# One ring of six PSUM banks, and a DFT-47 on 64x64 tiles with constants per frequency slot

## The chip, the cores and the metric

The kernel runs on one core of a Trainium2 chip. What counts is the device time of one execution in microseconds (us), the median of several runs.

The core's engines work side by side, each through its own queue in order, and wait for one another by semaphores. TensorE (PE in the rows; PEld is its weight load) multiplies; VectorE (DVE), ScalarE (ACT) and GpSimd (POOL) do the elementwise work; SyncE (SP) issues most transfers, and POOL issues some. A transfer or an instruction that waits holds up all that stands behind it in the same queue.

## What is computed

The input x is 8 x 3008 x 256. Along the sequence of 3008 it goes through a real FFT, a complex 256x256 product with bias and a soft threshold, and the inverse FFT. What comes out goes through a feed-forward layer whose gate is h cos(h):

```python
X = np.fft.rfft(x, axis=1)
Yr = Xr @ w_r - Xi @ w_i + b_r
Yi = Xr @ w_i + Xi @ w_r + b_i
Yr = np.sign(Yr) * np.maximum(np.abs(Yr) - lam, 0.0)
Yi = np.sign(Yi) * np.maximum(np.abs(Yi) - lam, 0.0)
y = np.fft.irfft(Yr + 1j * Yi, n=3008, axis=1)
h = y @ w_in            # 256 -> 2048
g = h * np.cos(h)
out = g @ w_out         # 2048 -> 256
```

## The kernel before

**The transform.** Since 3008 = 64 * 47, the FFT is a DFT-64 and then a DFT-47, with indices permuted on the host so that no twiddle factors stand between them. For each batch b there are three stages. `stage_a(b)` loads x in six chunks (tile `xt`), folds mirrored halves on POOL into sums (`xe`) and differences (back into `xt`), and makes the DFT-64 in three bursts of matmuls into `pa`, two chunks to a burst. ACT copies `pa` out to `ao`, and the result goes to DRAM (`scr1`). `stage_b(b)` works on four quarters q of eight frequency slots each:

- `load(q)` brings the tile `at` back from `scr1`.
- `forward(q)` makes the DFT-47: 16 matmuls of K = 24 by M = 32, 512 columns wide, into four banks `pb`. Each of the four h (cosine or sine part of real or imaginary part) has one block of 24 rows, and one and the same 24x32 constant serves all slots. DVE transposes the four banks back over `at`, and the tile goes through DRAM (`scrF`) to the tile `z`, which brings channels onto the partitions.
- `combine(q)` has POOL add and subtract the four parts of `z` to make real and imaginary spectrum (`x`, L519), patch slot 0 when q is 0 (L524 to L527), and multiply by signs (L532). ACT casts each to float32r (`Xh`, L513), DVE or POOL takes the rest (`Xl`), and the sum of both parts, for a three-product complex multiplication, gets the same treatment.
- `wmix(q)` is that complex product: 36 matmuls into six banks `pw` one after another, with bias and threshold on ACT and DVE; its `fold` brings the result through `tr` and DRAM (`scrT`) to the tile `y`.
- `inverse(q)`, for b > 0 through `spread(q)`, makes the inverse DFT-47 into four banks `pi`, copied by ACT to `bo` and stored to `scr2`.

`stage_c(b, t)` loads one of six column tiles back (`bt`), makes the inverse DFT-64 into `pc` and splits the result in two float32r parts, `xTh` and `xTl`.

**The feed-forward layer.** `moe_step(b, t, f)` runs for 8 batches, 6 column tiles and 16 blocks f of 128 hidden channels, 768 steps in all. One step has six matmuls into `ph`; then ACT and DVE in turn make h cos(h) (L812, L813, L815, L816: `u`), ACT casts (L817: `gh`), and DVE or, for two f of four, POOL takes the rest (`gl`, helpers `rest` L286 and `rest_pool` L283). `second` is the product with w_out: six matmuls into `po`, four of `gh` and two of `gl`; it is written three steps behind (`SKEW = 3`, four buffers of `gh` and `gl`).

**Order.** The Fourier stages of batch b+1 (and `stage_a` of b+2) are generators; each `moe_step` of batch b pulls from them twice, as many yields as a budget allows (`A_COST`, `B_COST`, `C_COST`, from `PAIR`, `QUAD`, `READ`). `weave` puts `stage_a` between the yields of `stage_b`, one yield to every `A_EVERY`; `GAP` sets the distance of the last `stage_c`. A scheduler then sets the order on each engine.

**Banks.** Two of the eight PSUM banks hold `po`. Tag "h" has two banks for `ph`, tag "f" four for all Fourier products (`BANKS`, L41):

```python
ph = ps.tile([128, 512], F32, tag="h", name="ph", bufs=BANKS["h"])
```

A matmul that starts a tile waits until the readers of the tile that had the bank before are through. So a step's `ph` waits for the last reader, L816, of the `ph` two steps back. `burst` makes the first of a group of matmuls wait for all four banks at once, so that the rest runs without waits.

**Staging buffers.** `stage_out` gives one of three buffers (tag "ao") to `ao`, `bo` and `ob`; `tr` has a buffer of its own. `z`, `at` and `y` have one buffer each.

Of the kernel before, what the change touches and what calls it, by code (L numbers as in the profile page):

```python
# [38 lines left out]
GAP = 7  # L39
A_EVERY = 5  # L40
BANKS = dict(f=4, h=2)  # L41
PAIR, QUAD, READ = 1.15, 1.25, 0.3
# [30 lines left out]
def _constants():  # L73
# [66 lines left out]
    cs = np.zeros((4, 32, 32))  # L140
    rows = np.arange(24).reshape(2, 6, 2).transpose(1, 0, 2).reshape(-1)
    cs[:2, :24, :24] = C[rows, :24]
    cs[2:, :24, :24] = S[rows, :24]
    cs = cs.reshape(128, 32)
    c_sig = np.concatenate([np.ones((48, 32)), sig.T]).astype(np.float32)
    c_ff = np.concatenate([f1, ei, fa, cs], 1).astype(np.float32)
# [4 lines left out]
    return [np.ascontiguousarray(a) for a in (c_sig, c_f3, c_ff, c_if, c_iw, c_sgn)]  # L151
# [3 lines left out]
def tile_body(ctx: ExitStack, tc, x, w_r, w_i, b_r, b_i, w_in, w_out,  # L155
              c_sig, c_f3, c_ff, c_if, c_iw, c_sgn, out):
# [10 lines left out]
    ff = cp.tile([128, 352], F32, name="ff")  # L167
# [68 lines left out]
    def split_f64(hi, lo, raw):  # L236
# [53 lines left out]
    banks = []  # L290

    def fps(name):
        if "pro" in pool:
            if not banks:
                banks.extend("fhf")
            tag = banks.pop(0)
            return ps.tile([128, 512], F32, tag=tag, name=name, bufs=BANKS[tag])
# [6 lines left out]
    def drained(p, ins):  # L304

        for q, readers in (side if "pro" in pool else ring)[-8:]:
            if q is p:
                readers.append(ins.ins)
# [16 lines left out]
    def burst(m, calls, loads=()):  # L325
# [5 lines left out]
        kept, n = (side, 2) if "pro" in pool else (ring, BANKS["f"])  # L331
# [70 lines left out]
    def stage_a(b):  # L402
# [20 lines left out]
        for c0 in range(0, 6, at_once):  # L423
# [10 lines left out]
            for c in cs:  # L434
# [9 lines left out]
                del ld[c], ev[c]  # L444
                load(c + 2)
            yield PAIR * at_once


    def stage_b(b):
# [17 lines left out]

        def load(q):
            if b and q < 4:
                at[q] = wk.tile([128, 2048], F32, tag="at", name="at", bufs=1), []  # L470
                for h in range(4):
                    ins = nc.sync.dma_start(at[q][0][32 * h:32 * h + 24].rearrange("j (s d) -> j s d", s=8),
                                            scr1[b][h // 2, :, 8 * q:8 * q + 8, h % 2])
                    at[q][1].append(ins)
                    if b == 1 and q == 0:
                        behind(ins, mark["pc"], "first tile")
# [486 lines left out]
```

## Time and profile before

| | us |
|---|---|
| median of 3 runs | 2814.15 (2811.34 to 2817.79) |
| the profiled execution, its own time | 2816.3 |
| its span, first to last instruction | 2814.5 |
| PE busy in the span | 2657.7 (94%) |
| DVE busy | 1901.3 (68%) |
| ACT busy | 1668.3 (59%) |
| POOL busy | 1204.0 (43%) |

The mean granted TensorE clock of the execution is 0.976 of full speed. Up to about 120 us the Fourier stages of batch 0 run alone; from then to about 2480 us feed-forward steps and Fourier stages run side by side; the rest is the feed-forward layer of the last batch. Each of the seven batches 1 to 7 has four `pb` bursts, four `pi` bursts and 24 `pw` products; there are 21 `pa` bursts. A busy span in a row is what the record says of one instruction; matmuls overlap, so what one costs PE is read from the start of one to the start of the next.

### The profile page before, as it was taken

What the parts mean: (1) busy time and instruction counts of PE and PEld (TensorE: products, weight loads), DVE (VectorE), ACT (ScalarE), POOL (GpSimd) and SP (SyncE); (2) the same over time, 40 slices, a digit from 0 to 9 for tenths busy, and PEclk for the clock granted to TensorE, in tenths of its full rate; (3) what the DMA queues carried; (4) which work ended last, traced back from release to release, by engine and by line L of the source; (5) the groups of instructions that cost most, each with busy time, mean ns of one, the idle gap of its engine ahead of it and who ended that gap; (6) DMA issues with size and microseconds to landing.
All of it is one profiled execution on the core that took longest, in us unless ns stands there. A gap on an engine that the chain in (4) does not pass through costs nothing. (4 is left out here: it accounts for less than half of the span.)

```text
span 2814.5 us, 36916 instructions
## 1 busy us (share of the span) xinstructions
PE 2657.7 (94%) x13161; PEld 2110.6 (75%) x13161; DVE 1901.3 (68%) x2912; ACT 1668.3 (59%) x2964; POOL 1204.0 (43%) x1111
## 2 busy tenths in 40 slices
PE   8789999999999999989999999999999999999999
PEld 6467677777787777867778777787777777788888
DVE  6586675677756676666766767567676677766665
ACT  5465555566566555655556556565565656666666
POOL 5455652355423654245532556226552344422222
PEclk9899989999999999999999999999999999999999
DMA  5434533256304453044431445314542234310000
GB/s 178 123 110 130 156 106 90 65 139 175 107 24 119 128 150 98 30 120 135 135 90 39 118 128 150 83 49 116 141 113 76 56 86 123 111 49 29 8 15 15
DMA packets 169801, 275.42 MB, mean 98 GB/s; under 512 B 14064, under 2 KB 112896, under 8 KB 166032
## 3 DMA queue, kind: packets, MB, share of 16 engines
q1 hardware_dynamic: 160832, 243.78, 31.0%
q0 software_dynamic: 7792, 27.96, 3.2%
q8 instruction: 104, 1.70, 0.3%
q10 hardware_dynamic: 992, 1.31, 0.2%
q14 instruction: 81, 0.66, 0.1%
HBM read 142.45 MB, written 130.55 MB: 97 GB/s over the span
## 5 line engine op out<-in xcount | busy, mean ns | idle before, releaser
L283 POOL TENSOR_TENSOR gl<-u,gh 128x512 fp32r<-128x512 f32 (+1 forms) x384 | 512.7, 1335 | 1177.3 <-ACT gh L817 1017.6
L813 DVE SCALAR_TENSOR_TENSOR u<-ph,u 128x512 f32<-128x512 f32 (+1 forms) x768 | 515.9, 673 | 311.6 <-ACT u L812 310.1
L816 DVE TENSOR_TENSOR u<-ph,u 128x512 f32<-128x512 f32 (+1 forms) x768 | 518.5, 676 | 292.3 <-ACT u L815 275.4
L815 ACT ACTIVATE u<-u 128x512 f32<-128x512 f32 (+1 forms) x768 | 478.4, 624 | 384.7 <-DVE u L813 383.2
L812 ACT ACTIVATE u<-ph 128x512 int32<-128x512 f32 (+1 forms) x768 | 450.8, 589 | 352.2 <-PE ph L807 345.8
L805 PE MATMUL ph<-xTh,win 128*128 128x512 f32 (+1 forms) x1536 | 616.7, 402 | 45.1 <-DVE u L816 41.9
L787 PE MATMUL po<-gh,wout 128*128 128x512 f32 (+1 forms) x1536 | 607.2, 395 | 3.1 <-ACT ob L795 2.6
L806 PE MATMUL ph<-xTl,win 128*128 128x512 f32 (+1 forms) x1536 | 600.6, 391 | 0.3 <-DVE xTl L773 0.3
L788 PE MATMUL po<-gh,wout 128*128 128x512 f32 (+1 forms) x1536 | 600.1, 391 | 0.0
L807 PE MATMUL ph<-xTh,win 128*128 128x512 f32 (+1 forms) x1536 | 599.8, 390 | 0.0
L817 ACT CAST gh<-u 128x512 fp32r<-128x512 f32 (+1 forms) x768 | 468.1, 610 | 213.5 <-DVE u L816 210.5
L791 PE MATMUL po<-gl,wout 128*128 128x512 f32 (+1 forms) x1536 | 494.2, 395 | 45.1 <-POOL gl L283 39.9
L805 PEld LDWEIGHTS ph<-xTh,win 128*128 128x128 f32 x1536 | 291.4, 190 | 164.9 <-DVE u L816 86.3
L286 DVE TENSOR_TENSOR gl<-u,gh 128x512 fp32r<-128x512 f32 (+1 forms) x384 | 332.8, 867 | 104.8 <-ACT gh L817 101.3
L791 PEld LDWEIGHTS po<-gl,wout 128*128 128x128 f32 x1536 | 286.7, 190 | 119.3 <-POOL gl L283 49.1
L787 PEld LDWEIGHTS po<-gh,wout 128*128 128x128 f32 x1536 | 292.8, 191 | 84.2 <-ACT gh L817 5.8
L807 PEld LDWEIGHTS ph<-xTh,win 128*128 128x128 f32 x1536 | 292.1, 190 | 58.0
L788 PEld LDWEIGHTS po<-gh,wout 128*128 128x128 f32 x1536 | 293.0, 191 | 53.5
L806 PEld LDWEIGHTS ph<-xTl,win 128*128 128x128 f32 x1536 | 292.4, 190 | 49.6 <-DVE xTl L773 0.8
L519 POOL TENSOR_TENSOR x<-z 128x384 f32<-128x384 f32 x112 | 125.8, 1157 | 58.2 <-DMA z<-scrF 43.2
L286 DVE TENSOR_TENSOR Xl<-x,Xh 128x768 fp32r<-128x768 f32 x56 | 87.3, 1559 | 58.5 <-ACT Xh L513 58.3
L767 PEld LDWEIGHTS pc<-ff,bt 128*128 128x128 f32 x768 | 100.3, 196 | 29.3 <-issue 17.2
(118 smaller groups left out, 2671.6 us busy)
## 6 DMA issues: line engine op xcount, KB each, us to landing
scrF<-at SPq DMA_DIRECT2D x28, 1024.0 KB
z<-scrF SPq DMA_DIRECT2D x112, 256.0 KB
scrT<-tr SPq DMA_DIRECT2D x56, 512.0 KB
y<-scrT SPq DMA_DIRECT2D x112, 256.0 KB
bt<-scr SPq DMA_DIRECT2D x94, 256.0 KB
scr<-bo SPq DMA_DIRECT2D x124, 192.0 KB
scr<-ao SPq DMA_DIRECT2D x84, 256.0 KB
at<-scr SPq DMA_DIRECT2D x112, 192.0 KB
```

Source lines behind the costliest of these rows:

```text
L283: return nc.gpsimd.tensor_tensor(out=lo, in0=x, in1=hi.bitcast(F32), op=ALU.subtract)
L787: mm(po[e][:, :n], wo[0][:, 0, f, es], gh[:, :n], start=f == 0, stop=False)
L788: mm(po[e][:, :n], wo[0][:, 1, f, es], gh[:, :n], start=False, stop=False)
L791: mm(po[e][:, :n], wo[0][:, 0, f, es], gl[:, :n], start=False, stop=f == NFC - 1)
L805: mm(h, win[:, 0, c, fs], th[:, c, :n], start=c == 0, stop=False)
L806: mm(h, win[:, 0, c, fs], tl[:, c, :n], start=False, stop=False)
L807: mm(h, win[:, 1, c, fs], th[:, c, :n], start=False, stop=c == 1)
L812: nc.scalar.activation(k[:, :n], h, AF.Identity, bias=0.25, scale=1.0 / TWO_PI)
L813: nc.vector.scalar_tensor_tensor(out=u[:, :n], in0=h, scalar=1.0 / TWO_PI, in1=k[:, :n], op0=ALU.mult, op1=ALU.subtract)
L815: nc.scalar.activation(u[:, :n], u[:, :n], AF.Sin, bias=HALF_PI, scale=TWO_PI)
L816: nc.vector.tensor_tensor(out=u[:, :n], in0=h, in1=u[:, :n], op=ALU.mult)
L817: nc.scalar.copy(gh[:, :n], u[:, :n])
```

## The change

All of the six banks go into one ring, tag "f": `ph` is taken from it by `fps` like any Fourier tile, and its last reader, now L821, is noted by `drained`. `burst` still waits for four banks at once, now out of six.

`forward` works with 64x64 tiles. The constants `fq` are different for each of the 32 slots, hold half sums and half differences of the DFT's columns with their signs and slot 0's special case, and are loaded for each quarter by POOL's queue (28 loads of 256 KB). Real and imaginary rows lie together (K = 48), sixteen matmuls of 256 columns go to the four banks, two to each part of a bank. `load(q)` places the rows accordingly, in six transfers instead of four for q = 0.

`combine` no longer adds, patches or multiplies by signs: ACT casts straight from `z`, in halves (six casts of 384 elements in place of three of 768), DVE takes four rests, POOL makes the sum in two halves and takes its two rests.

`stage_a` loads the next chunks one yield later; `tr` comes from `stage_out`, as a fourth user of its three buffers; `wm` moves into `z`'s tag. The numbers that space the stages change.

```diff
-GAP = 7
-A_EVERY = 5
-BANKS = dict(f=4, h=2)
-PAIR, QUAD, READ = 1.15, 1.25, 0.3
+GAP = 9
+A_EVERY = 10
+BANKS = 6
+SLOTS = ((0, 0), (1, 1), (0, 1), (1, 0))
+SLOT0 = ((0, 0), (0, 1), (1, 1), (1, 0))
+PAIR, QUAD, READ = 1.0, 2.1, 0.7
...
-        m = wk.tile([128, 512], F32, tag="tr", name="wm", bufs=1)
-        aq = wk.tile([128, 2, 512], F32, tag="z", name="wa", bufs=1)
-        a, q = aq[:, 0], aq[:, 1]
+        maq = wk.tile([128, 3, 512], F32, tag="z", name="wa", bufs=1)
+        m, a, q = (maq[:, j] for j in range(3))
...
     def fps(name):
-        if "pro" in pool:
...
-        p = ps.tile([128, 512], F32, tag="f", name=name, bufs=BANKS["f"])
-        ring.append((p, []))
+        if len(ring) >= BANKS:
+            assert ring[-BANKS][1]
+        p = ps.tile([128, 512], F32, tag="f", name=name, bufs=BANKS)
+        if "pro" not in pool:
+            ring.append((p, []))
         return p
...
                 del ld[c], ev[c]
+            yield PAIR * at_once
+            for c in cs:
                 load(c + 2)
-            yield PAIR * at_once
+            yield 0.5
...
         def load(q):
             if b and q < 4:
-                at[q] = wk.tile([128, 2048], F32, tag="at", name="at", bufs=1), []
+                fq = wk.tile([128, 512], F32, tag="fq", name="fq", bufs=2)
+                with tc.issue_after(mark["x0"].ins) if b == 1 else ExitStack():
+                    loads = [nc.gpsimd.dma_start(fq, c_fq[:, 512 * q:512 * q + 512])]
+                t = wk.tile([128, 2048], F32, tag="at", name="at", bufs=1)
...
-            burst(4, [((p[h][32 * w:32 * w + 32], ff[32 * h:32 * h + 24, 320:352], t[32 * h:32 * h + 24, 512 * w:512 * w + 512]),
-                       dict(start=True, stop=True, skip_group_check=True)) for w in range(4) for h in range(4)], loads)
+            burst(4, [((p[2 * e + g][64 * v:64 * v + 64, 256 * j:256 * j + 256],
+                        fq[64 * g:64 * g + 48, 64 * i:64 * i + 64], t[64 * g:64 * g + 48, 256 * i:256 * i + 256]),
+                       dict(start=j == 0, stop=j == 1, skip_group_check=True))
+                      for e in range(2) for j in range(2) for v in range(2) for g in range(2) for i in (4 * v + 2 * e + j,)], loads)
...
-            for r, even, odd, ops in ((0, 0, 3, (ALU.add, ALU.subtract)), (1, 1, 2, (ALU.subtract, ALU.add))):
...
-                    po.tensor_tensor(out=xv[..., 24 * k:24 * k + 24], in0=zv[:, even][..., k:k + 24],
-                                     in1=zv[:, odd][..., k:k + 24], op=op)
...
+            for r in range(2):
+                for v in range(2):
+                    nc.scalar.copy(hi[r][:, v], z[:, r, v])
+                    yield 0.2
+                    rest(lo[r][:, v], z[:, r, v], hi[r][:, v])
+                    yield 0.3
+            for v in range(2):
+                nc.gpsimd.tensor_tensor(out=z[:, 0, v], in0=z[:, 0, v], in1=z[:, 1, v], op=ALU.add)
+                yield 0.6
+                nc.scalar.copy(hi[2][:, v], z[:, 0, v])
+                yield 0.2
+                rest_pool(lo[2][:, v], z[:, 0, v], hi[2][:, v])
+                yield 0.5
...
-            tr = wk.tile([128, 4, 8, 32], F32, tag="tr", name="tr", bufs=1)
+            yield 0.8
+            tr = stage_out("tr").rearrange("p (j s e) -> p j s e", j=4, s=8)
...
         yield from forward(0)
-        yield 4.5
+        yield 6.5
         yield from combine(0)
...
-        yield 5.0
+        yield 9.0
         yield from inverse(3)
...
-        yield 3.5
+        yield 6.0
         for hf in range(2):
             p = fps("pc")
...
-        ph = ps.tile([128, 512], F32, tag="h", name="ph", bufs=BANKS["h"])
+        ph = fps("ph")
...
-        nc.vector.tensor_tensor(out=u[:, :n], in0=h, in1=u[:, :n], op=ALU.mult)
+        drained(ph, nc.vector.tensor_tensor(out=u[:, :n], in0=h, in1=u[:, :n], op=ALU.mult))
```

What this does to the order is shown at three places. The first is PE late in a batch, where feed-forward steps run alone; the steps' `ph` are numbered 13025, 13061, 13083 before and 13011, 13033, 13055, 13091 in the change, and a step's `gh` has a number 8 above its `ph`. Before:

```order
L806 MATMUL ph_13083<-xTl_12520,win_81 128x448
L807 MATMUL ph_13083<-xTh_12519,win_81 128x448
L787 MATMUL po0_12990<-gh_13033,wout_1052 128x448
L788 MATMUL po0_12990<-gh_13033,wout_1052 128x448
L787 MATMUL po1_12991<-gh_13033,wout_1052 128x448
L788 MATMUL po1_12991<-gh_13033,wout_1052 128x448
```

The same place in the change:

```order
L811 MATMUL ph_13091<-xTl_12528,win_81 128x448
L812 MATMUL ph_13091<-xTh_12527,win_81 128x448
L792 MATMUL po0_12998<-gh_13019,wout_1044 128x448
L793 MATMUL po0_12998<-gh_13019,wout_1044 128x448
L792 MATMUL po1_12999<-gh_13019,wout_1044 128x448
L793 MATMUL po1_12999<-gh_13019,wout_1044 128x448
```

Behind the `ph` of a step stood the product of two steps back; now the product of three steps back stands there.

The second is ACT at the first combine of a batch (the rows on `u` and `gh` are the feed-forward steps' own work). Before:

```order
L812 ACTIVATE u_10421<-ph_10414 128x512
L817 CAST gh_10379<-u_10378 128x512
L815 ACTIVATE u_10421<-u_10421 128x512
L513 CAST Xh_10523<-x_10522 128x768
L812 ACTIVATE u_10458<-ph_10451 128x512
L817 CAST gh_10422<-u_10421 128x512
```

In the change:

```order
L817 ACTIVATE u_10510<-ph_10503 128x512
L822 CAST gh_10489<-u_10488 128x512
L532 CAST Xh_10541<-z_10441 128x2x8x24 x4
L820 ACTIVATE u_10510<-u_10510 128x512
L817 ACTIVATE u_10532<-ph_10525 128x512
L539 CAST Xh_10541<-z_10441 128x2x8x24
```

ACT's cast stood behind POOL's sums, five steps after the `pb` burst; now four casts in a row take `z` itself, four steps after it.

The third is POOL where `stage_a` loads and folds its chunks, behind the first `pa` burst of a batch. Before:

```order
L410 DMA xt_10882<-in_0_dram 128x1024
L283 TENSOR_TENSOR gl_10688<-u_10686,gh_10687 128x512
L410 DMA xt_10889<-in_0_dram 128x1024
L416 TENSOR_TENSOR xe_11061<-xt_10882 128x512
L417 TENSOR_TENSOR xt_10882<-xt_10882 128x2x256
L416 TENSOR_TENSOR xe_11102<-xt_10889 128x512
L417 TENSOR_TENSOR xt_10889<-xt_10889 128x2x256
L283 TENSOR_TENSOR gl_10768<-u_10766,gh_10767 128x512
```

In the change:

```order
L416 DMA xt_11135<-in_0_dram 128x1024
L416 DMA xt_11137<-in_0_dram 128x1024
L422 TENSOR_TENSOR xe_11325<-xt_11135 128x512
L423 TENSOR_TENSOR xt_11135<-xt_11135 128x2x256
L293 TENSOR_TENSOR gl_11030<-u_11028,gh_11029 128x512
L422 TENSOR_TENSOR xe_11571<-xt_11137 128x512
L423 TENSOR_TENSOR xt_11137<-xt_11137 128x2x256
```

The folds still stand right behind their own loads; a `gl` now stands between the two folds here, and at the batch's other two `pa` bursts all four folds stand in a row.

## Rows read from the trace of the kernel before

**Rows 1.** Stretches: length; PE, PEld, DVE, ACT, POOL busy (count); clock, DMA share, GB/s.
```profile
0.00:200.00 200.00, 162.68 (x761) 114.59 (x762) 138.86 (x208) 105.09 (x192) 102.54 (x100) 0.91 0.47 140
200.00:2500.00 2300.00, 2184.82 (x10973) 1733.23 (x10973) 1569.10 (x2409) 1357.61 (x2405) 1030.04 (x954) 0.98 0.38 105
2500.00:2814.00 314.00, 310.17 (x1430) 262.72 (x1428) 193.38 (x297) 205.59 (x369) 71.43 (x57) 1.00 0.06 19
```

**Rows 2.** Waits of PE, 200 to 2500 us: total us, times, longest us.
```profile
PE po L791 <- POOL gl L283: 39.7, 17, 6.1
PE ph L805 <- DVE u L816: 34.7, 37, 2.7
PE pc L767 <- DMA bt<-scr: 12.8, 7, 2.8
PE pi L328 <- DMA y<-scrT: 11.4, 6, 2.2
PE pi L328 <- DVE xTl L773: 3.5, 1, 3.5
...
PE pw L582 <- ACT bo L657: 2.5, 1, 2.5
```

**Rows 3.** Two stretches around a wait of PE for y, columns as in Rows 1.
```profile
1100.00:1104.00 4.00, 2.08 (x13) 0.98 (x15) 1.60 (x3) 1.38 (x3) 1.26 (x1) 0.90 0.74 203
1104.00:1108.00 4.00, 4.00 (x19) 1.91 (x12) 1.33 (x2) 3.18 (x6) 0.00 (x0) 0.67 0.16 35
```

**Rows 4.** Timeline of PE, one pb burst: start us, length us, instruction.
```profile
1229.39 0.61 PE L328 MATMUL pb<-at,ff 24*32 24x512 f32 x1
...
1230.46 0.50 PE L805 MATMUL ph<-xTh,win 128*128 128x512 f32 x1
```

**Rows 5.** Timeline of PE and its weight loads, one pa burst.
```profile
1243.43 0.61 PE L328 MATMUL pa<-xt,ff 64*64 64x512 f32 x1
...
1243.45 0.13 PEld L328 LDWEIGHTS pa<-xt,ff 64*64 64x64 f32 x1
...
1243.88 0.59 PE L328 MATMUL pa<-xt,ff 64*64 64x512 f32 x1
...
1245.30 0.50 PE L805 MATMUL ph<-xTh,win 128*128 128x512 f32 x1
```

**Rows 6.** Groups by shape: xcount, busy us, mean ns, idle before.
```profile
L519 POOL TENSOR_TENSOR x<-z 128x384 f32<-128x384 f32 x112 | 125.8, 1157 | 58.2 <-DMA z<-scrF 43.2 <-DVE tr L635 10.9 <-issue 3.2
...
L286 DVE TENSOR_TENSOR Xl<-x,Xh 128x768 fp32r<-128x768 f32 x56 | 87.3, 1559 | 58.5 <-ACT Xh L513 58.3
...
L513 ACT CAST Xh<-x 128x768 fp32r<-128x768 f32 x56 | 46.8, 835 | 55.1 <-POOL x L525 27.3 <-POOL x L532 22.0 <-POOL x L519 5.8
```

**Rows 7.** Timeline of PE, start of the first pb burst of a batch.
```profile
1188.55 0.61 PE L328 MATMUL pb<-at,ff 24*32 24x512 f32 x1
```

**Rows 8.** Timeline of POOL, ACT and PE at the combine behind it.
```profile
1205.93 3.95 POOL L519 TENSOR_TENSOR x<-z 128x384 f32<-128x384 f32 x4 [5.48 <-DMA z<-scrF]
...
1210.24 0.83 ACT L513 CAST Xh<-x 128x768 fp32r<-128x768 f32 x1 [4.39 <-POOL x L525]
...
1211.80 0.73 PE L791 MATMUL po<-gl,wout 128*128 128x512 f32 x2 [3.05 <-POOL gl L283]
```

**Rows 9.** Timeline of POOL: load of two x chunks, their folds, the rest behind.
```profile
1244.85 0.61 POOL L410 DMA_DIRECT2D xt<-in_dram  x1 [5.98 <-PE pa L338]
...
1255.30 1.28 POOL L416 TENSOR_TENSOR xe<-xt 128x512 f32<-128x512 f32 x1 [8.01 <-DMA xt<-in_dram]
...
1261.13 1.26 POOL L283 TENSOR_TENSOR gl<-u,gh 128x512 fp32r<-128x512 f32 x1
```

**Rows 10.** Timeline of PE, the wait for that rest.
```profile
1262.44 0.79 PE L791 MATMUL po<-gl,wout 128*128 128x512 f32 x1 [6.11 <-POOL gl L283]
```

**Rows 11.** DMA issues: count, KB each, median us from issue to landing.
```profile
xt<-in_dram POOLq DMA_DIRECT2D x36, 512.0 KB, 7.8
```

**Rows 12.** Waits of ACT in the whole span, columns as in Rows 2.
```profile
ACT bo L657 <- DMA scr<-ao: 15.1, 5, 7.0
```

More of the change, by code (lines that the diff above doesn't have):

```diff
@@ L304, in drained @@
     def drained(p, ins):
-        for q, readers in (side if "pro" in pool else ring)[-8:]:
+        for q, readers in (side if "pro" in pool else ring)[-BANKS:]:
             if q is p:
@@ L466, in stage_b @@
         at = {}
+        at = {}
         def load(q):
             if b and q < 4:
-                at[q] = wk.tile([128, 2048], F32, tag="at", name="at", bufs=1), []
+                fq = wk.tile([128, 512], F32, tag="fq", name="fq", bufs=2)
+                with tc.issue_after(mark["x0"].ins) if b == 1 else ExitStack():
+                    loads = [nc.gpsimd.dma_start(fq, c_fq[:, 512 * q:512 * q + 512])]
+                t = wk.tile([128, 2048], F32, tag="at", name="at", bufs=1)
                 for h in range(4):
[L472 to L476, printed above, removed]
+                    own = q == 0 and SLOT0[h] != SLOTS[h]
+                    r0 = 64 * (h // 2) + 24 * (h % 2)
+                    for (v, r), s0, s1 in ((SLOT0[h], 0, 1), (SLOTS[h], 1, 8)) if own else ((SLOTS[h], 0, 8),):
+                        ins = nc.sync.dma_start(t[r0:r0 + 24, 256 * s0:256 * s1].rearrange("j (s d) -> j s d", d=256),
+                                                scr1[b][v, :, 8 * q + s0:8 * q + s1, r])
+                        loads.append(ins)
+                        if b == 1 and q == 0:
+                            behind(ins, mark["pc"], "first tile")
+                at[q] = t, fq, loads
@@ L491, in forward @@
+            turned = t.rearrange("p (a g c e s k) -> p e g s c a k", a=4, g=2, c=2, e=2, s=2)
+            for e in range(2):
+                for g in range(2):
+                    pv = p[2 * e + g]
+                    drained(pv, nc.vector.transpose(turned[:, e, g], pv.rearrange("p (s c a k) -> p s c a k", s=2, c=2, a=4)))
+                    if e == 0 or g == 0:
+                        yield Hold(READ)
             f = dr.tile([128, 2048], F32, tag="scrF", name=f"scrF_{b}_{q}")
@@ L522, in combine @@
-            if q == 0:
-                z0 = zv[:, :, :2, 0, :24]
-                po.tensor_copy(x[:, 0, 0, :, 0, :24], z0[:, 0])
-                po.tensor_copy(x[:, 0, 0, :, 0, 24:], z0[:, 1, :, :24])
-                po.tensor_scalar(out=x[:, 1, 0, :, 0, :24], in0=z0[:, 2], scalar1=-1.0, scalar2=None, op0=ALU.mult)
-                po.tensor_copy(x[:, 1, 0, :, 0, 24:], z0[:, 3])
-            xr, xi = (x[:, r].rearrange("p w c s k -> p (w c s k)") for r in range(2))
-            cast(0, xr, rest)
@@ L530, in combine @@
-            for c in range(2):
-                xv = x[:, 1, :, c].rearrange("p w s k -> p w (s k)")
-                po.tensor_tensor(out=xv, in0=xv, in1=sgn[:, 8 * q:8 * q + 8].rearrange("p (w s) k -> p w (s k)", w=4), op=ALU.mult)
-            yield 0.8
-            cast(1, xi, rest)
-            t1 = z[:, :768]
-            po.tensor_tensor(out=t1, in0=xr, in1=xi, op=ALU.add)
-            yield 0.8
-            cast(2, t1, rest_pool)
-            yield 0.8
+            for r in range(2):
[4 more added lines that the diff above has]
+                    yield 0.3
@@ L608, in wmix @@
                 if b:
-                    fold(q, e)
+                    yield from fold(q, e)
         Y = {}
```

66 lines of the change are left out of this document (29 added, 37 removed).

## The prediction

> **What bounds the kernel now.** I read the stretches first. Between 200 and 2500 us, where feed-forward steps and Fourier stages run together, PE is busy 2184.8 of 2300 us; DVE, the next, has 1569.1 [rows 1]. In the last 314 us, with no Fourier work left, PE has 310.2 us for 1430 matmuls at full clock, 0.217 us each: six of them, one product of a step, are 1.30 us, the unit that I count with below. So PE sets the end, and a change can win only what PE loses: 115.2 us of idle time in the middle stretch, and 2% of its clock, 46 us [rows 1].
>
> Who ends that idle time is in the waits of PE [rows 2]: 39.7 us for the rest `gl` from POOL, 34.7 us in 37 waits of a step's `ph` for L816, the last reader of the bank two steps back, 12.8 and 11.4 us for the loads `bt` and `y`. Waits of about 2 us cost more than themselves: behind a wait for `y` at about 1101 us the granted clock is 0.90 and then 0.67 in two stretches of 4 us, 0.4 + 1.3 = 1.7 us of full speed, PE being at its lower level, 1.2 GHz, for part of them [rows 3].
>
> **The change, part by part.** The sum is made against the profiled execution, 2816.3 us.
>
> *The DFT-47 bursts.* A `pb` burst of 4x4 tiles takes PE from 1229.39 to 1230.46, 1.07 us [rows 4]. The new one has four tiles at once, as a `pa` burst has: with eight passes of 256 columns where `pa` has four of 512. A `pa` burst takes 1243.43 to 1245.30, 1.87 us, with 0.45 us from the first pass to the second [rows 5]. The columns per tile are the same, so I take 1.87 us: 28 bursts x 0.80 = **+22.4 us**, all on PE. That is also the lower bound. The upper: each of the eight passes shows its weight load of 0.13 us [rows 5], 8 x 0.13 x 28 = 29 us more. I take none of it, since the weights of the second pass are loaded at 1243.45, while the first pass, from 1243.43, is in the same rows of the array.
>
> The Trainium skill says otherwise (TensorE: Matmul & The Clock Gate, Part 3, What overlaps and what doesn't): a weight load overlaps a running matmul only when their row groups differ. By that rule this term would be 51 us and not 22, and the weight load in the row above could not have started there; the trace speaks against it, at least for passes of 512 columns.
>
> *The ring.* A `ph` now takes the bank of the sixth tile back. In the feed-forward alone the order shows the product of three steps back behind a `ph`, where that of two steps back stood: PE has one whole step more, two products of 1.30 us, before it needs what DVE and ACT make. The 37 waits for L816 are 0.9 us each, 2.7 at most [rows 2], so nearly all fit in that. But a late chain also makes `gl` late, which PE meets a step later. I take four fifths: **-28 us** (bounds 0 and -34.7). With six banks the burst that waited 3.5 us for `xTl`, a reader of a bank of its ring, and the 2.5 us of `pw` behind `bo` [rows 2], go too: **-6 us**.
>
> *The distances.* The last inverse of a batch now has 9 units of yields ahead of it and not 5, each `bt` load 6 and not 3.5, and `GAP` is 9. PE's work between load and use grows by some steps of 2.6 us, while these waits are at most 2.2 and 2.8 us [rows 2]. Both go: 11.4 + 12.8 = **-24 us**. PE fills the time with feed-forward steps, which are there anyway.
>
> *The combine.* POOL loses four sums of 1.157 us per quarter [rows 6], the sign products and slot 0's patches, while the sum of both parts and its rest are cut in two. That is more than 28 x 4.6 = 130 us off POOL, none of it on PE's path unless a `gl` is queued behind. ACT has six casts at half the size in place of three of 0.835 us, DVE four rests for two of 1.559 us [rows 6]: about even. What matters is who waits for `z`. At a batch's first combine the burst starts at 1188.55 [rows 7], POOL has `z` at 1205.93, 17.4 us later, ACT its sums at 1210.24, and PE, behind the `gl` that POOL had queued behind the sums, goes on at 1211.80 after 3.05 us [rows 8]. Now ACT's own queue stops for `z`: with a burst longer by 0.8 us it goes on 18.2 us after the burst's start, then makes four casts (0.42 to 0.84 us each), a sine and a cast of the step it held back, with DVE's product between: about 4 us, 22 us in all. PE reaches the product that needs this after the burst (1.9) and 13 units (16.9), 18.8 us. It waits about 3 us, as before: **0** at seven batches. At the other quarters the order puts 8 to 10 steps between burst and casts, over 22 us, and nobody waits.
>
> *POOL's own loads.* The folds still stand right behind the load of their chunks. Before, POOL issued the load at 1244.85, stood until 1255.30, folded, and started the `gl` behind at 1261.13 [rows 9]; PE had waited 6.11 us when it went on at 1262.44 [rows 10]. A load lands in 7.8 us in the median [rows 11], 7.35 from the burst's end. At the first of a batch's three bursts the order now puts `gl` after one fold (two sums of 1.3): 7.35 + 2.6 + 1.3 = 11.3 us, while PE has 7.2 units and six `pw`, 10.4 us, until it needs it. At the second and third all four sums come first, 13.9 us against 12.0 and 13.3. That is 0.9 + 1.9 + 0.6 = 3.4 us a batch, some 20 us for six batches. Before, the 39.7 us for POOL's `gl`, less seven first combines of 3, leave the same 19: **0** (bounds -20 and, with the longest landing, +50).
>
> *The clock.* The waits that go are 58 of 115.2 us, so half of the 46 us would come back; many are short, so **-20 us** (bounds -5 and -30).
>
> *New waits.* `tr` is now in the ring of three staging buffers, and 146 uses of it become 202. ACT waited there 15.1 us in five waits, 7.0 at the longest [rows 12], and in the new order an `ao` follows two steps behind the `bo` whose buffer it takes. ACT and DVE have over 700 us of slack each in the middle stretch [rows 1], but a wait of several us reaches PE. The constants add 28 loads to POOL's queue, at 0.61 us of issue [rows 9]. I take **+10 us** for all (bounds 0 and +40).
>
> Sum: 22.4 - 28 - 6 - 24 - 20 + 10 = -46 us, or 2770 us. The profiled execution lies 2 us above the median of the runs, so 2769 us.
>
> **The rivals.**
> *Slower: POOL's loads land late.* The folds wait for their own load at 18 places, and two thirds of them now have no `gl` between. If loads land 10 us after the burst, as at 1255.30 [rows 9], each place costs 2.65 us more, 48 us, and the clock takes 20 more: -46 + 68 = +22, **2836 us**. It decides from about 9.5 us on. For it: more transfers, packed closer. Against it: the median of 7.8 us [rows 11].
> *Waits that only move.* The `ph` waits are not for banks but for a late chain of DVE and ACT, and PE stops at `gl` in place of `ph`. Then a third of that term is left, 20 us less, and the clock gives 8 less: **2797 us**. For it: the chain is the same length. Against it: the extra step.
> *Weight loads show.* 29 us more: **2798 us**; only the shorter pass speaks for it. The rule of the Trainium skill named above (TensorE: Matmul & The Clock Gate, What overlaps and what doesn't) would give this.
> *Better: POOL's relief counts.* With POOL free earlier the waits for `gl` lose 20 us, the clock 10 more, and no new waits come: **2729 us**.
> *The waits come back elsewhere*, all of them: about **2814 us**.
>
> **How the numbers follow.** The forecast has 0.50, the late loads 0.10, moving waits 0.15, weight loads 0.08, the better case 0.12, nothing gained 0.05. The range leaves out the late loads and half of the better case: 2735 to 2815 us. A measurement can tell about 0.2% (5.6 us) from no change. Faster by more than that are the forecast, the better case and the two in between, 0.85, less 0.06 for their tails: 0.79; same 0.09; slower 0.12.
>
> **What would show it.** In the profile after: `pb` bursts of 1.9 us (2.9 if weight loads show); hardly a wait of PE at `ph` for `u`, and none at `pi` or `pc` for transfers; waits at `po` for `gl` of 40 us still, in the two groups of places; POOL's busy time down by 130 us or more; granted clock about 0.985. I am wrong if the waits for `gl` rise by what those for `ph` fall, if ACT shows long waits at `Xh` beyond the first quarter, or if POOL's waits for `xt` exceed 8 us in most places.

## The result, and the profile after

The changed kernel takes 2713.0 us in the median (2710.9 to 2715.3), the kernel before 2816.0 beside it: a ratio of 0.9635, with an interval of 0.9616 to 0.9653. That is 103 us less; I had forecast 46, and 2735 as the low end. The direction was right, the size was not.

The stretches of the changed kernel, columns as in [rows 1]:

```profile
0.00:200.00 200.00, 163.89 (x767) 116.45 (x767) 138.38 (x207) 108.42 (x195) 100.83 (x101) 0.89 0.46 140
200.00:2400.00 2200.00, 2146.48 (x10963) 1747.80 (x10964) 1574.85 (x2473) 1363.91 (x2494) 870.68 (x844) 0.99 0.39 113
2400.00:2711.00 311.00, 306.10 (x1433) 261.21 (x1431) 189.75 (x289) 201.18 (x360) 69.89 (x56) 1.00 0.07 22
```

About as many matmuls (10,963 after, 10,973 before) fit into a middle stretch shorter by 100 us. PE is idle for 53.5 us of it, against 115.2, and POOL is busy 160 us less. The ends, ahead of and behind it, are as they were, within 3 us.

The waits of PE in the middle stretch, to set beside [rows 2]:

```profile
PE po L792 <- ACT gh L822: 13.7, 7, 3.0
PE pi L334 <- DMA y<-scrT: 9.6, 6, 4.5
PE pa L334 <- issue: 7.6, 6, 1.3
PE pa L334 <- PE po L796: 4.0, 4, 1.0
PE po L796 <- POOL gl L293: 3.5, 3, 1.7
```

No `ph` waits for `u` in this stretch any more, no `pc` for `bt`, and 3.5 us are left of the 39.7 for POOL's `gl`, which I had expected to stay. The largest rest is 2 us at the first combine of each of seven batches, now for `gh`.

PE at one `pb` burst, to set beside [rows 4], and the first weight loads of its first tile:

```profile
1161.40 0.43 PE L334 MATMUL pb<-at,fq 48*64 48x256 f32 x1
...
1161.68 1.69 PE L344 MATMUL pb<-at,fq 48*64 48x256 f32 x27
1163.29 0.50 PE L810 MATMUL ph<-xTh,win 128*128 128x512 f32 x1
```

```profile
1161.40 0.13 PEld L334 LDWEIGHTS pb<-at,fq 48*64 48x64 f32 x1 [0.35 <-DVE u L821]
...
1161.46 0.13 PEld L334 LDWEIGHTS pb<-at,fq 48*64 48x64 f32 x1
```

The burst takes 1161.40 to 1163.29, 1.89 us, where I had taken 1.87: 28 x 0.82 = 23 us more on PE, as forecast (27 of the 28 bursts take 1.89 us, one 1.96). The second weight load starts at 1161.46, while the first pass, from 1161.40, is in the same rows.

**Where the 103 us came from.** PE's idle time over the whole span falls from 156.8 to 95.1 us: 62. Its clock, summed over stretches of 4 us as (1 - granted clock), loses 67.9 us before and 35.4 after: 32. The bursts take 23 back. That leaves 32 us more to find. A wait costs more than its idle time: ahead of it the last matmul runs 0.39 us where the next would have started after 0.23, and behind it the first takes 0.34 to the second (1180.92, 1182.65 and 1182.99 in the changed kernel), 0.16 + 0.11 = 0.27 us. PE's timeline has 113 waits before and 61 after, so by this estimate 14 us. The other 18 I can't place.

### The profile page after: what moved, and what is told of

The parts are those of the page before. It is cut to its first block, busy times and chain, and to the rows that moved or that the text cites. A ratio compares the mean times of both kernels' runs of the same rounds, so it can differ in the third digit from the quotient of the medians.

```text
span 2711.6 us, 37067 instructions
## 1 busy us (share of the span) xinstructions
PE 2616.5 (96%) x13161; PEld 2125.5 (78%) x13161; DVE 1903.0 (70%) x2968; ACT 1673.5 (62%) x3048; POOL 1041.4 (38%) x999
## 4 chain that ended last, share of the span: by engine, by line
PE 76%; DVE 11%; DMA 7%; ACT 3%; issue 2%; POOL 1%; SPq 1%; ACTq 0%; DVEq 0%; POOLq 0%
PE ph L810 11%; PE ph L811 10%; PE ph L812 10%; PE po L796 10%; PE po L792 10%; PE po L793 10%; PE pc L772 3%; DVE Xl L296 2%; DMA z<-scrF 2%; PE pw L585 2%; PE pw L586 2%; PE pw L587 2%; DVE u L821 1%; DMA y<-scrT 1%; DMA scrF<-at 1%
## 5 line engine op out<-in xcount | busy, mean ns | idle before, releaser
L293 POOL TENSOR_TENSOR gl<-u,gh 128x512 fp32r<-128x512 f32 (+1 forms) x384 | 500.5, 1304 | 1264.1 <-ACT gh L822 1060.2
L821 DVE TENSOR_TENSOR u<-ph,u 128x512 f32<-128x512 f32 (+1 forms) x768 | 518.3, 676 | 228.0 <-ACT u L820 211.6
L792 PE MATMUL po<-gh,wout 128*128 128x512 f32 (+1 forms) x1536 | 599.8, 391 | 15.3 <-ACT gh L822 13.7
L810 PE MATMUL ph<-xTh,win 128*128 128x512 f32 (+1 forms) x1536 | 602.8, 393 | 6.5 <-DVE u L821 6.5
L793 PE MATMUL po<-gh,wout 128*128 128x512 f32 (+1 forms) x1536 | 593.6, 387 | 2.7 <-DVE wout L266 2.7
L812 PE MATMUL ph<-xTh,win 128*128 128x512 f32 (+1 forms) x1536 | 595.9, 388 | 0.0
L796 PE MATMUL po<-gl,wout 128*128 128x512 f32 (+1 forms) x1536 | 482.6, 389 | 6.0 <-POOL gl L293 3.5
L792 PEld LDWEIGHTS po<-gh,wout 128*128 128x128 f32 x1536 | 288.6, 188 | 82.2 <-ACT gh L822 20.7
L793 PEld LDWEIGHTS po<-gh,wout 128*128 128x128 f32 x1536 | 288.7, 188 | 54.3 <-DVE wout L266 3.4
L296 DVE TENSOR_TENSOR gl<-u,gh 128x512 fp32r<-128x512 f32 (+1 forms) x384 | 292.0, 760 | 33.7 <-ACT gh L822 28.7
L296 DVE TENSOR_TENSOR Xl<-z,Xh 128x384 fp32r<-128x384 f32 x112 | 110.9, 1029 | 29.0 <-ACT Xh L532 29.0
L585 PE MATMUL pw<-Xh,wf 128*128 128x384 f32 x336 | 113.9, 339 | 0.2 <-ACT Xh L539 0.2
L586 PE MATMUL pw<-Xh,wf 128*128 128x384 f32 x336 | 113.7, 338 | 0.0
```

What stands on the lines that cost most here:

```text
L293: return nc.gpsimd.tensor_tensor(out=lo, in0=x, in1=hi.bitcast(F32), op=ALU.subtract)
L296: return nc.vector.tensor_tensor(out=lo, in0=x, in1=hi.bitcast(F32), op=ALU.subtract)
L792: mm(po[e][:, :n], wo[0][:, 0, f, es], gh[:, :n], start=f == 0, stop=False)
L793: mm(po[e][:, :n], wo[0][:, 1, f, es], gh[:, :n], start=False, stop=False)
L796: mm(po[e][:, :n], wo[0][:, 0, f, es], gl[:, :n], start=False, stop=f == NFC - 1)
L810: mm(h, win[:, 0, c, fs], th[:, c, :n], start=c == 0, stop=False)
```

## Experiments: the three parts, alone and in pairs

The change has three parts that can be told apart: the ring (R), the distances (S: `GAP`, `A_EVERY`, yields, costs, the place of the loads in `stage_a`), and the new forward stage (F: 64x64 tiles, `fq`, the combine, `tr` in the staging ring). Six runs complete the table. Each is compared with runs of the kernel before on the same chip. That kernel takes 2810.8 to 2816.4 us there, so a difference between the plain times of two runs is open by up to 6 us.

**e1, the ring alone.**

```
-BANKS = dict(f=4, h=2)
+BANKS = 6
...
-        ph = ps.tile([128, 512], F32, tag="h", name="ph", bufs=BANKS["h"])
+        ph = fps("ph")
...
+        drained(ph, nc.vector.tensor_tensor(out=u[:, :n], in0=h, in1=u[:, :n], op=ALU.mult))
```

> The kernel before with the ring of six banks alone: `ph` takes its bank from the ring, and all else (distances, tiles, combine) is as before. Two theories of the 36 us of waits for POOL's `gl` that I had left at nothing and that are gone after the change. Relief: they went because the new combine takes the sums off POOL. Then the ring alone wins only the waits of `ph` for `u` (28) with 6 more for other banks and about 12 of clock, 46 in all: 2769 us, and PE still waits 35 to 45 us for POOL's `gl`. Slack: they went because the ring puts the product of a step one step later on PE, 2.6 us, and most of the waits for `gl` are shorter than that. Then the ring alone wins these too, with about 12 more of clock: 2722 to 2735 us, and waits for POOL's `gl` under 15 us.

Measured: 2851.1 against 2816.4, ratio 1.012 (1.0099 to 1.0141). Slower; both theories missed. Waits of PE, whole span, from here on total us, times, longest us:

```profile
PE po L787 <- POOL gl L283: 50.8, 26, 4.9
PE po L783 <- ACT gh L813: 21.9, 22, 2.4
PE pw L578 <- ACT Xh L509: 20.9, 10, 2.8
...
PE ph L801 <- DVE u L812: 11.5, 4, 4.4
```

The waits of `ph` fall from 41.9 to 11.5, as the term said. But PE stops at `gl`, `gh` and `Xh` instead.

**e2, the distances alone.**

```
-GAP = 7
-A_EVERY = 5
+GAP = 9
+A_EVERY = 10
...
-        yield 5.0
+        yield 9.0
         yield from inverse(3)
```

Not all distances grow: the yields between a combine and its products fall from 3.0 (first of a batch) and 2.0 to 1.5.

> The kernel before with the distances alone: `GAP` 9, `A_EVERY` 10, the longer yields of `stage_b` and `stage_c`, the new costs, the loads of the x chunks behind the yield; two banks of their own for `ph`, the old tiles and combine. Both theories (POOL's relief by the new combine, one more step of slack by the ring) leave the waits for POOL's `gl` at 35 to 45 us here. The waits for `bt` and `y` go, 20 us, with 5 to 8 us of clock: 2786 to 2792 us. If the distances are what took the waits for `gl` (the folds of the x chunks stand farther behind their loads), the time is about 2745 us and these waits are under 15 us.

Measured: 2814.8, ratio 0.9996 (0.9985 to 1.0006): nothing. The waits they were for are still there, so my reading of them was wrong:

```profile
PE pc L771 <- DMA bt<-scr: 24.5, 9, 4.7
PE pi L328 <- DMA y<-scrT: 13.7, 7, 2.5
```

**e3, the new forward stage alone** (the diff's hunks of `_constants`, `load`, `forward`, `combine`, and `tr = stage_out("tr")`).

> The kernel before with the new forward stage alone: 64x64 tiles with the constants `fq`, the combine on ACT and DVE, `tr` in the staging ring; old banks and distances. The bursts cost 28 x 0.82 = 23 us more. Relief of POOL: the waits for its `gl` fall from 40 to under 10 us, with 12 us of clock: 2793 to 2800 us. Slack by the ring: they stay at 35 to 45 us, and the time is 2836 to 2842 us, slower than before.

Measured: 2856.2, ratio 1.0137 (1.0116 to 1.0159). The waits for POOL's `gl` go, but others come that cost more:

```profile
PE po L792 <- ACT gh L822: 44.4, 13, 8.4
PE ph L810 <- DVE u L821: 38.5, 32, 8.3
PE pw L587 <- ACT Xh L541: 22.9, 13, 3.9
...
PE po L796 <- POOL gl L293: 2.5, 4, 1.6
```

**e4, the change without the new forward stage** (R and S: those hunks taken back).

> The changed kernel with the old forward stage: 32x32 tiles, POOL's sums and sign products in the combine, `tr` in a buffer of its own; the ring of six and the distances are those of the change. The bursts are 23 us shorter. Relief of POOL: the waits for its `gl` come back, 30 to 40 us, with 12 us of clock: 2730 to 2742 us, slower than the changed kernel. Slack by the ring: they stay under 10 us, and the time is 2688 to 2695 us, faster than the changed kernel.

Measured: 2877.9, ratio 1.0211 (1.0189 to 1.0234): the slowest of the eight combinations, 165 us above the changed kernel. PE's idle time is 115.6 us longer than there, the clock loses 49.9 us more, 86 more waits cost 23 by the estimate above, and the bursts save 23: 165 us.

```profile
PE po L791 <- POOL gl L283: 47.1, 31, 5.8
PE pw L580 <- ACT Xh L511: 35.1, 21, 2.9
```

**e5, the change without the ring** (S and F: `BANKS = dict(f=4, h=2)` and `ph` with a tag of its own).

> The changed kernel with the old banks, two for `ph` and four for the rest; tiles and distances as in the change. So far the ring alone cost 35 us, the tiles alone 40, and both together with the distances win 103, so parts work on each other. If ring and tiles need each other (the tiles make ACT's chain of a step late at a combine, and only six banks let PE run on), the time is 2840 to 2860 us, with 30 us or more of waits of `ph` for `u` and of `po` for `gh`, as with the tiles alone. If the distances are what makes the tiles good, it is under 2760 us and the waits for `gh` are under 20 us.

Measured: 2860.4 against 2810.8, ratio 1.0181 (1.0156 to 1.0206). The first theory, at the edge of its range, except that the waits stand at `ph`, not at `gh`:

```profile
PE ph L814 <- DVE u L825: 92.5, 37, 8.6
```

**e6, the change without the distances** (R and F: all yields, `GAP`, `A_EVERY` and costs as before).

> The changed kernel with the old distances (`GAP` 7, `A_EVERY` 5, the old yields and costs, the loads of the x chunks ahead of the yield). If ring and tiles need each other and the distances only place the loads, as their run alone says (0 us), the time is 2713 plus some 24 us for `bt` and `y` and a little clock, 2735 to 2750 us. If all three parts are needed, it is over 2790 us and the waits at the combine (`pw` for `Xh`, `po` for `gh`) are 30 us or more.

Measured: 2737.0, ratio 0.9734 (0.9717 to 0.9752), within the first range. But of the waits for `bt` and `y` that the range was made from, only 7.1 us are there:

```profile
PE pa L334 <- issue: 17.4, 5, 4.2
PE po L792 <- DVE gl L296: 14.4, 7, 3.2
PE po L788 <- ACT gh L818: 11.3, 11, 1.9
...
PE pc L768 <- DMA bt<-scr: 3.6, 1, 3.6
```

The whole table, us against the kernel before on the same chip:

| | without F | with F |
|---|---|---|
| neither R nor S | 0 | +40 |
| S | -2 | +50 |
| R | +35 | -74 |
| R and S | +62 | -103 |

**The waits for POOL's `gl` go with F alone.** Over the whole span they are 39.9 us in the kernel before, 50.8 with R, 32.5 with S and 47.1 with both; with F, in the same order, 2.5, 5.9, 4.1 and 3.5. So "Relief" in the expectations of e1 to e4 is right about these waits; what it had wrong is the time, since alone F brings other waits that cost more.

**Ring and new stage pay only together.** Why the new stage needs the ring is seen at the first combine of a batch. ACT, then PE, without the ring (e5), burst at 1189.71:

```profile
1209.84 1.75 ACT L536 CAST Xh<-z 128x384 fp32r<-128x384 f32 x4 [7.16 <-DMA z<-scrF]
...
1214.59 0.62 ACT L826 CAST gh<-u 128x512 fp32r<-128x512 f32 x1 [1.59 <-DVE u L825]
```

```profile
1214.61 0.79 PE L814 MATMUL ph<-xTh,win 128*128 128x512 f32 x1 [8.55 <-DVE u L825]
```

and in the changed kernel, burst at 1161.40:

```profile
1177.14 1.76 ACT L532 CAST Xh<-z 128x384 fp32r<-128x384 f32 x4 [2.79 <-DMA z<-scrF]
...
1181.98 0.62 ACT L822 CAST gh<-u 128x512 fp32r<-128x512 f32 x1 [1.66 <-DVE u L821]
```

```profile
1182.65 0.50 PE L792 MATMUL po<-gh,wout 128*128 128x512 f32 x1 [1.34 <-ACT gh L822]
```

The new combine makes ACT stand in its own queue for `z`, 7.16 us in e5, and the steps behind come to a halt. With two banks for `ph`, PE then stops 8.55 us here and 6.3 to 8.6 us in each of seven batches (6.0 to 8.4 in e3); with six it has steps enough in hand and loses 1.34 us here and 1.2 to 3.0 in the seven (1.1 to 1.9 in e6). (In e5 `z` also comes later, 20.1 us after the burst and not 15.7; the output store of a tile runs beside it there.)

Why the ring needs the new stage is seen in e4, where POOL still makes the sums. POOL, ACT and PE at one combine:

```profile
1300.71 5.22 POOL L517 TENSOR_TENSOR x<-z 128x384 f32<-128x384 f32 x4 [0.94 <-POOL st L629]
1305.89 1.26 POOL L283 TENSOR_TENSOR gl<-u,gh 128x512 fp32r<-128x512 f32 x1
1307.12 2.23 POOL L530 TENSOR_TENSOR x<-x,sgn 128x384 f32<-128x384 f32 x2
1309.43 1.82 POOL L534 TENSOR_TENSOR z<-x 128x768 f32<-128x768 f32 x1
1312.20 1.82 POOL L283 TENSOR_TENSOR Xl<-z,Xh 128x768 fp32r<-128x768 f32 x1 [0.94 <-ACT Xh L511]
```

```profile
1309.39 0.84 ACT L511 CAST Xh<-x 128x768 fp32r<-128x768 f32 x1 [2.92 <-POOL x L530]
```

```profile
1304.61 0.50 PE L787 MATMUL po<-gh,wout 128*128 128x512 f32 x1 [1.13 <-ACT gh L817]
1307.21 1.22 PE L791 MATMUL po<-gl,wout 128*128 128x512 f32 x2 [1.40 <-POOL gl L283]
...
1312.17 0.69 PE L580 MATMUL pw<-Xh,wf 128*128 128x384 f32 x1 [1.18 <-ACT Xh L511]
```

POOL works 13.3 us on one combine, with a `gl` in the midst of it, and PE stops three times within 8 us. The order shows why it has nothing to do meanwhile: with ring and old stage, four products of steps (309 to 312) stand in a row ahead of the first `pw`, and the next `ph` behind it; in the kernel before, `pw` stands between steps that go on.

## Experiments: what of the old stage the ring can't bear

**e7, POOL's sums put back as work.** Ahead of the casts of the changed kernel:

```
+            x = wk.tile([128, 2, 2, 2, 8, 24], F32, tag="st", name="x", bufs=1)
+            for r in range(2):
+                for v in range(2):
+                    nc.gpsimd.tensor_tensor(out=x[:, r, v], in0=z[:, r, v], in1=z[:, r, v], op=ALU.add)
+                    yield 0.4
```

> The changed kernel with POOL's four sums of a combine put back as work alone: each quarter POOL adds the four halves of `z` to themselves into `x`, which nobody reads; the order is made with them. 112 x 1.16 = 130 us more on POOL. If POOL's time is what kept the changed kernel from being as slow as the one without the new tiles (2878 us), because its `gl` are queued behind, the waits for `gl` come back, 30 us or more, and the time is over 2770 us. If it is the chain from `z` through POOL to ACT's casts, this kernel stays within 15 us of 2713.

Measured: 2744.6 against 2810.8, ratio 0.9764 (0.9747 to 0.978). Neither: 32 us lost, but only 5.0 of waits for POOL's `gl`.

**e8, the sums as a chain**: as e7, and ACT, DVE and POOL read `x` in place of `z`.

> As the run with POOL's sums put back as work alone, but with the chain too: ACT's casts, the rests and the last sum read the `x` that POOL made (the constants are halved, so that the numbers are those of the change). If the chain through POOL is the cause, the time is that of the changed kernel without the new tiles less its shorter bursts, 2850 to 2900 us, with 20 us or more of waits of `pw` for `Xh`. If POOL's time is the cause, it is as the run with the work alone, over 2770 us and within 15 us of it. If neither, within 15 us of 2713: then the 32x32 bursts of the old forward stage or what else it has (sign products, slot 0) are to blame.

Measured: 2708.8, ratio 0.9632 (0.9613 to 0.9652): as fast as the change, with POOL's 112 sums back. So taking these sums off POOL wins no time on balance. It does take waits: 18 us of those for `gl` are back. But `gh` waits 8.6 us in place of 13.7 and `y` 3.2 in place of 9.6, and PE's idle time in all is 90.2 us against 95.1. That the work without the chain (e7) is slower than with it stays unexplained; e7 waits 24.9 us for `gh` and 15.1 for `Xh`.

```profile
PE po L801 <- POOL gl L293: 21.9, 16, 3.5
PE po L797 <- ACT gh L827: 8.6, 12, 1.1
```

**e9, e4 with more distance in the combine** (`yield 0.8` three times to 1.6, `yield 1.5` behind `combine` to 4.0, the costs with them). This also takes back what S had cut there.

> The kernel with the ring and the distances but the old forward stage (2878 us) once more, with more distance in the combine: 2.4 more units of yields within it and 2.5 more between it and its products, so that its work on POOL, 12 us, stands before some 9 units of other work and not 6. If the old combine only stands too close to its products, the waits of `pw` for `Xh` fall from 35 to under 8 us and the time is under 2790 us. If the old chain stops ACT's and DVE's own queues wherever its products stand, the time stays over 2840 us.

Measured: 2803.0 against 2814.9, ratio 0.996 (0.9945 to 0.9975): 75 us better than e4, not the 88 asked for, with `pw` waiting 5.0 us for `Xh` in place of 35.1.

**e10, e4 with the casts in halves.**

```
+                for v in range(2):
+                    s = slice(384 * v, 384 * v + 384)
+                    nc.scalar.copy(hi[:, s], src[:, s])
+                    take(lo[:, s], src[:, s], hi[:, s])
```

> The kernel with the ring and the distances but the old forward stage (2878 us), with the casts, the rests and the last sum of the old combine cut into halves of 384, as the new combine has them. If the grain of the combine is what the ring needs (ACT, DVE and POOL work on halves side by side), the time is under 2790 us. If not, it stays within 20 us of 2878.

Measured: 2883.3, ratio 1.0243 (1.0207 to 1.028): nothing. The grain is not it.

**e11, e4 without sign products and slot 0's patches** (those lines of `combine` deleted; this part of the computation is left out).

> The kernel with the ring and the distances but the old forward stage (2878 us), without the sign products and slot 0's patches on POOL: this part of the computation is left out, so 28 x 2.2 us less on POOL, between the sums and ACT's second cast. If the length of POOL's chain ahead of the casts is the cause, half of the loss comes back: under 2800 us. If not, it stays over 2850 us.

Measured: 2828.2, ratio 1.0053 (1.0035 to 1.0072): 50 us better than e4, between the two.

**e12, e8 with two more sums a quarter** (`x[:, 1, v] + x[:, 1, v]` ahead of the casts).

> The changed kernel with POOL's chain of sums (2709 us) and two more sums a quarter where the old combine had its sign products (the constants are scaled, so that the numbers are those of the change): POOL's work ahead of the casts is then as long as in the old combine. If the length of that chain is the cause of the loss without the new tiles, the time is over 2780 us. If not, it stays under 2725 us, and what is left is the grain of the casts, the short bursts or `tr`.

Measured: 2737.6, ratio 0.9723 (0.9694 to 0.9752): 29 us slower than e8, with `pw` waiting 20.5 us for `Xh`. Between the two again: the length counts, but it is not all.

**e13, e4 with `tr` in the staging ring** (`tr = stage_out("tr")`).

> The kernel with the ring and the distances but the old forward stage (2878 us), with `tr` in the ring of three staging buffers as in the change, in place of a buffer of its own. ACT waits there 34 us for the store of an `ao` before it can fill a `bo`, and PE 13 us for that `bo`; the changed kernel has neither. If the order of the staging ring is the cause, these waits fall under 10 and 4 us and the time is 2850 to 2862 us. If not, it stays within 10 us of 2878.

Measured: 2843.4 against 2812.7, ratio 1.0104 (1.0072 to 1.0137): 35 us better than e4, but not by the waits I named; ACT's are 35.1 us, against 33.9. What else `tr` does there is open.

**e14, e4 with e9, e11 and e13 together.**

> The kernel with the ring and the distances but the old forward stage (2878 us), with all three at once: more distance in the combine (alone 75 us), no sign products and slot 0's patches (alone 50 us; this part of the computation is left out), `tr` in the staging ring. If the loss of the old stage is the length of POOL's chain against its distance, and no more, the gains add up to 2725 to 2755 us. If something else of the old stage costs under the ring (its 32x32 bursts, its layout), the time stays over 2775 us.

Measured: 2748.7, ratio 0.9771 (0.9743 to 0.9799): 129 of the 165 us come back, fewer than the 160 of the three added, and within the range. The old bursts being 23 us shorter, some 59 us of what the new stage gives remain unplaced.

## Experiments: the waits that are left

**e15, the first combine of a batch farther** (`yield 6.5` behind `forward(0)` to 9.0).

> The changed kernel with the first combine of a batch 2.5 units farther behind its burst (9 and not 6.5), about one step. PE waits there 13.7 us in all seven batches, 2 us each. If it is distance alone, these waits fall under 4 us and the time is 2695 to 2704 us, with the clock of seven dips. If the later combine only makes `y` or `bt` late at the end of the batch, the time stays within 5 us of 2713.

Measured: 2709.1, ratio 0.9629 (0.9604 to 0.9653), the second theory. The waits moved:

```profile
PE pi L334 <- DMA y<-scrT: 27.2, 10, 4.8
PE po L792 <- ACT gh L822: 7.5, 4, 2.9
```

**e16, the same in e8.**

> The changed kernel with POOL's chain of sums (2709 us), where POOL and not ACT stands for `z`, with the first combine 2.5 units farther behind its burst. It waits 21.9 us at `gl` and 8.6 at `gh`, most of it at first combines. If it is distance alone, the time is 2682 to 2692 us, the fastest of all; if the later combine makes other loads late, within 5 us of 2709.

Measured: 2735.7, ratio 0.9722 (0.9696 to 0.9748), 27 us slower than e8. `gl` falls from 21.9 to 4.6 us, but `gh` rises from 8.6 to 26.4: a miss of both theories.

**e17, distance for `y` alone.**

```
             if q < 3:
                 yield from forward(q + 1)
+            else:
+                yield 2.5
...
-        yield 9.0
+        yield 11.5
         yield from inverse(3)
```

> The changed kernel with more distance for `y` alone: 2.5 units in the last quarter, where no forward stage stands between, and 11.5 units and not 9 ahead of the last inverse. The waits of `pi` for `y` are 9.6 us, most of them in the first batch. If they are distance alone, they fall under 4 us: 2703 to 2709 us. If what is gained there is lost at the next combine, which comes later in its batch, the time stays within 4 us of 2713.

Measured: 2682.4 against 2812.4, ratio 0.9544 (0.953 to 0.9558): 30 us better than the change, far more than the 5 us of `y` that went; both theories missed:

```profile
PE po L794 <- ACT gh L824: 11.3, 6, 2.9
PE pa L334 <- issue: 8.0, 2, 6.1
...
PE pi L334 <- DMA y<-scrT: 4.3, 2, 2.4
```

PE is idle 74.0 us in all, 41 waits in place of 61: many short ones, which no line of the list shows as large, went with it. Idle time falls by 21.1 us, the clock's loss by 3.2, and 20 waits fewer are 5.4 by the estimate above: the 30 us. The cost `B_COST` rises by the same 5.0 units, as by 2.5 in e15 and e16, so the pace of the other Fourier work changes too; no run holds it apart from the distance for `y`.

**e18, both distances.**

> The changed kernel with both: the first combine 2.5 units farther, as in the run that gave 2709 us, and 2.5 units more ahead of the last two inverses of a batch, since that run waits 27 us for `y`. If distance is all, the waits for `y` fall under 6 us and those for `gh` stay at 7.5: 2682 to 2692 us with the clock of ten dips. If waits only move from one load to the next, the time stays over 2703 us.

Measured: 2679.1, ratio 0.9524 (0.9511 to 0.9537), the fastest of all, below both ranges: 133 us less than the kernel before on the same chip, with PE busy 2610.4 of 2678.2 us. Its lead over e17 is within the spread of the two.

## Why the prediction was wrong, by its own steps

The terms of the sum against the traces, in us. The middle stretch gives the waits (61.7 us of idle time less in all), the whole span the rest:

| term | forecast | measured |
|---|---|---|
| bursts | +22.4 | +23 |
| ring | -34 | -40.7 |
| distances | -24 | -14.6 |
| combine, first of a batch | 0 | -5.0 |
| POOL's loads: the other waits for its `gl` | 0 | -17.5 |
| new waits | +10 | +16.1 |
| clock | -20 | -32 |
| a wait beyond its idle time | no term | -14 (estimate) |
| not placed | no term | -18 |
| sum | -46 | -103 |

So of the missing 57 us some 32 had no term at all, 14 are idle time (17.5 at POOL's `gl`, the other terms together 4 the other way), and 12 are the clock.

- **The bursts, +22.4:** right, with the right reason. The Trainium skill (TensorE: Matmul & The Clock Gate, Part 3, What overlaps and what doesn't) would, by the estimate in the prediction, have 8 x 0.13 us of weight loads show, 2.9 us a burst; the 1.89 us and the load at 1161.46 speak against it here, for passes of 256 columns too.
- **The ring, -34:** the waits of `ph` went, all 34.7 us of the middle stretch, and with them the 6.0 at other banks; the size is right in the whole change. The step that failed is that I took the ring by itself: alone it costs 35 us. My rival "waits that only move" is what happens there, and with the extra step that I had set against it.
- **The distances, -24:** near in time by accident. With ring and new stage they are worth 29 us by the table of runs, but alone they give 2 and leave the waits for `bt` and `y`, while ring and new stage without them have 7.1 us of such waits. What they take away are waits of `pa` for issue (17.4 to 9.6) and of `po` for DVE's `gl` (14.4 to 2.3). In the whole change `bt` loses its 12.8 us and `y` goes from 11.4 to 9.6 only.
- **The combine, 0:** nearly right. At the first combines the waits for `gl` were 18.7 us; now `gh` waits there, 13.7 us, about 2 us each, not 3. I had z 17.4 us after the burst and ACT 18.2; it is 15.7. What I missed is that this rests on the ring: 6.0 to 8.6 us without it.
- **POOL's loads, 0: the largest term of idle time that failed.** Of the 39.7 us of waits for `gl`, 18.7 stood at the first combines. I put the rest down to the folds behind the loads. Of these 21.0 us only 15.0, in five waits, stood behind folds; 6.0, in five, stood behind POOL's sums at later combines, which I had not counted. All but 3.5 went. Those sums are gone from POOL. As to the loads, I had given one 7.35 us from the burst's end. In the changed kernel it lands in 5.3 us in the median, and in the middle stretch no fold waits over 3.9 us for it, where before it was up to 8.0 [rows 9]:

```profile
xt<-in_dram POOLq DMA_DIRECT2D x36, 512.0 KB, 5.3
```

```profile
1227.91 1.13 POOL L416 DMA_DIRECT2D xt<-in_dram  x2
1232.74 1.29 POOL L422 TENSOR_TENSOR xe<-xt 128x512 f32<-128x512 f32 x1 [3.71 <-DMA xt<-in_dram]
...
1235.36 1.76 POOL L293 TENSOR_TENSOR gl<-u,gh 128x512 fp32r<-128x512 f32 x1
```

The first row is the median of all such loads (count, KB, us from issue to landing); the rows below it are POOL behind the burst that answers to [rows 9]: it can fold 4.8 us after it issued the load, and the `gl` behind starts 2.6 us later, in time for PE. The loads land in 4.3 to 5.8 us in the four combinations with F and in 6.9 to 7.8 in the four without; why they land sooner, with more data moved, I have not shown. My better rival, "POOL's relief", gave 2729, the right sign and the right place: with the sums back on POOL (e8), 18 us of waits for `gl` are back. But the time is the same there, so these waits are not what the new stage's gain rests on.

- **The clock, -20:** 32. It follows the waits, and 14 us more of idle time went than I had summed.
- **New waits, +10:** 16, and not where I looked. ACT's waits for staging buffers, 15.1 us [rows 12], are gone from the list. But `pa` waits 7.6 us for issue, where it was 0.4, 4.0 behind `po` and 1.8 behind `u`, which it did not before.
- **What had no term:** I counted a wait at its idle time and its clock. By the estimate of 0.27 us each, 52 waits fewer are 14 us more; the other 18 stay open.

Under all of it lies the way I summed: each term was sized in the kernel before and added, as if the parts were independent. The table of runs shows parts of +35, -2 and +40 that make -103 together.

## What to carry to other kernels

A wait on an in-order engine says where the slack ends, not what it is worth: removing it alone may only bring the next wait to the front, so try the parts of a change in pairs before judging one. A shared ring of buffers gives PE more work in hand, but ties it to the slowest chain that fills the ring; shorten that chain, or give it distance, in the same edit. Once PE is idle under 4%, look at whole patterns of short waits and their clock: in e17 two yields, with the cost that goes with them, brought 30 us where the list named 5.

## What the runs showed of the hardware

Two short waits can cost more clock than time. In e4, behind the waits of 1.13 and 1.40 us above, four stretches of 4 us (columns as in [rows 1]):

```profile
1304.00:1308.00 4.00, 1.99 (x6) 1.37 (x7) 2.85 (x3) 1.71 (x4) 4.00 (x4) 0.80 0.90 212
1308.00:1312.00 4.00, 2.99 (x8) 1.78 (x6) 1.74 (x1) 1.55 (x2) 3.18 (x3) 0.50 0.27 50
1312.00:1316.00 4.00, 3.83 (x10) 3.25 (x11) 0.07 (x1) 0.28 (x2) 1.82 (x1) 0.50 0.00 0
1316.00:1320.00 4.00, 3.43 (x44) 2.23 (x43) 2.76 (x4) 2.17 (x4) 0.72 (x1) 0.92 0.01 4
```

PE runs at its lower level, 1.2 GHz, for two whole stretches: 0.8 + 2.0 + 2.0 + 0.3 = 5.1 us of full speed lost behind 2.5 us of waits (3.7 with the third, 1.18 us, which fell into the slow stretch). In the changed kernel the wait of 1.34 us at 1182.65 brings no dip: the granted clock stays at 1.00 in the stretches around it, and its matmuls go on 0.23 us apart.

The same load of 512 KB lands in 4.3 us in the median in e5, 5.3 in the changed kernel, 6.9 in e4 and 7.8 before. So a landing time read from one trace need not hold in a kernel with another order.
